# The third pair's attention weights transposed by the DMA engine inside the first block, and two later transfers moved behind stores

## The chip, the cores and the metric

One Trainium2 chip, one core. A core has TensorE (PE, the matmuls; its weight loads are listed apart as PEld), VectorE (DVE), ScalarE (ACT), GpSimd (POOL) and SyncE (SP, which issues nearly all DMA transfers here), and 16 DMA engines between the chip's memory and the core's on-chip memories SBUF and PSUM. Each engine works through its own list of instructions in order and waits at semaphores for the others. The metric is the device time of one execution in microseconds.

## The reference, cut to what matters

Two steps follow one another. Attention works on chunks of 64 tokens that see only themselves; a gated feed-forward layer (Mish) follows. Everything is float32.

```python
scores = scale * np.matmul(q_c, k_c.transpose(0, 1, 2, 4, 3))   # 8 batches, 8 heads, 9 chunks of 64 x 64
scores = scores - np.max(scores, axis=-1, keepdims=True)
attn = np.exp(scores)
attn = attn / (np.sum(attn, axis=-1, keepdims=True) + 1e-09)
out = np.matmul(attn, v_c)
...
h = x @ w_in                                   # x: 4608 tokens x 512; w_in: 512 x 2048
sp = np.where(h > 20.0, h, np.log1p(np.exp(np.minimum(h, 20.0))))
g = h * np.tanh(sp)
return (g @ w_out).astype(np.float32)          # w_out: 2048 x 512
```

## The kernel before, in words

The 4608 tokens are 36 tiles of 128; two tiles are a pair, 18 pairs in all, numbered from 0. A float32 factor of the large matmuls is split into an upper and a lower part ("hi" is a rounded copy by ACT, "lo" is the difference, made by DVE), and three matmuls stand for one.

**The first block.** The first eight tiles (pairs 0 to 3) go through two plain blocks of 16 slots each, slots 0 to 31. `prologue()` does the attention of pairs 0 and 1 and starts the first slots. Slot s of `slot()` issues to PE the up-projection of slot s+1 (`up`, tile h, line 389, 12 matmuls) and the down-projection of slot s-1 (`down`, tiles o, line 424, 12 matmuls), to ACT the Mish of slot s+1 (`mish`, line 401) and the upper part of slot s's activations (`g_hi`, line 406), and to DVE their lower part (`g_lo`, line 411). `down(s-1)` reads the lower part of slot s-1 first. In slots 0 to 15 the weights also have to be made: each slot loads two 512 KB tiles of raw weights over SP (`w("load")`, line 163), and ACT and DVE unpack and split them (`w_scale`, lines 170 and 179; `w_bits`, 192 and 193; `w_hi`, 205; `w_lo`, 211). `keep()` writes made weights back to memory.

The attention of pairs 2 and 3 lies between these steps; the table `softmax` says in which slot each step of which pair is issued: scores (`s`), maximum, exponential, sum with reciprocal (`a_inverse`, lines 310, 315, 318), division (`a_norm`, line 323, on DVE), transpose on PE (`a_transpose`, line 332, eight 128x128 tiles into PSUM) with a copy to SBUF by ACT (`a_copy`, line 342), and the product with the values (`a_values`, line 256, tile av), whose result ACT and DVE split into the block's x (`a_hi`, line 363; `a_lo`, line 366). Scores, transposes and values of one pair share one place in PSUM, so the next pair's transposes wait until `a_lo` has read the values. Pair 2 is divided in slot 8, transposed in slot 9 and multiplied in slot 10; pair 3 is transposed in slot 12 and multiplied in slot 13.

**The later blocks.** Four larger blocks of seven tiles each use a Strassen scheme: sets of 14 steps (`s_set`), in which PE alternates six matmuls of the up side (`s_up`, line 884) and six of the down side (`s_down`, tile d, line 1003). `s_out` adds the tile d to the totals in SBUF (line 1031, DVE) or, where a block begins anew, copies it there (line 1029, ACT). When a block is done, its totals go out in two groups of four stores (`s_store`, line 1047). Ten later pairs are spread over the sets by `plan_pair`. The distance from one pair's scores to its values decides between three plans: NEAR transposes on PE; MID and FAR let POOL separate the two 16-bit halves of each number (`p_split`, line 790), the DMA engine transpose them (`p_turn`, line 796, issued by SP), and POOL join them again (`p_join`, line 802). A pair has two such transfers, t = 0 and t = 1, of 128 x 1024 16-bit words. Two pairs follow FAR; their scores are at steps 92 and 204 and their second transfer is issued just ahead of the end of a block.

SP issues everything in one order, so a transfer also stands behind every transfer that was issued ahead of it.

## Time and profile before

| | |
|---|---|
| median of 3 runs | 795.67 us (794.31 to 795.96) |
| the profiled execution | 795.43 us, of which the span from the first to the last instruction is 793.6 us |
| PE busy | 780.8 us, 98% of the span |
| DVE busy | 591.8 us, 75% |
| ACT busy | 474.8 us, 60% |
| POOL busy | 302.7 us, 38% |
| q1, the queue of SP | 202.53 MB, 76.5% of the 16 DMA engines' span |

The difference between the profiled execution and its span, 1.8 us, is start and end, which the instructions don't show. A busy share is an average over stages in which different engines hold the others up; what a change is worth has to be read in the stage that it touches.

### The profile page before, as it was taken

How to read it: one execution, taken by the hardware profiler on the slowest of the kernel's cores; microseconds unless marked ns; L12 is line 12 of the kernel's file. 1: busy time of each engine (PE TensorE's matmuls, PEld its weight loads, DVE VectorE, ACT ScalarE, POOL GpSimd, SP SyncE). 2: the span in 40 equal slices, each digit the busy share in tenths (PEclk: the TensorE clock that was granted, in tenths of full speed). 3: DMA queues.
4: the chain of work that ended last, by engine and by line, in shares of the span. 5: the costliest groups of instructions: out<-in, count | busy, mean ns of one | idle time of the engine just before them, and what ended most of it. 6: DMA issues, size and time to landing. Idle time of an engine off the chain costs nothing.

```text
span 793.6 us, 15301 instructions
## 1 busy us (share of the span) xinstructions
PE 780.8 (98%) x5932; PEld 700.8 (88%) x5932; DVE 591.8 (75%) x929; ACT 474.8 (60%) x853; POOL 302.7 (38%) x263
## 2 busy tenths in 40 slices
PE   8999999999999999999999999999999999999996
PEld 7887888888889999999899999989999999999986
DVE  6898978888866776799577679976575897445666
ACT  5988865666676665555566466648464654544440
POOL 2000026556363236434434435454544453333340
PEclk9999999999999999999999999999999999999999
DMA  7698876989978868667978957788967667866537
GB/s 292 240 305 305 277 228 238 349 289 331 376 241 305 303 219 283 235 218 241 311 298 228 358 194 242 270 255 286 308 209 237 221 216 243 295 218 225 180 115 172
DMA packets 97224, 205.47 MB, mean 259 GB/s; under 512 B 26240, under 2 KB 49280, under 8 KB 89984
## 3 DMA queue, kind: packets, MB, share of 16 engines
q1 hardware_dynamic: 92864, 202.53, 76.5%
q10 hardware_dynamic: 4288, 1.97, 1.0%
q8 instruction: 47, 0.77, 0.4%
q14 instruction: 25, 0.20, 0.1%
HBM read 162.53 MB, written 38.80 MB: 254 GB/s over the span
## 4 chain that ended last, share of the span: by engine, by line
PE 76%; DVE 11%; ACT 6%; DMA 2%; issue 2%; SPq 1%; DVEq 0%; ACTq 0%
PE d L1003 29%; PE al L884 16%; PE g L884 8%; PE o_o L424 8%; PE h L389 7%; PE b L884 4%; PE av L256 2%; DVE sums L1031 2%; DVE sums L1034 1%; DMA out<-sums 1%; PE al L720 1%; DMA sums<-in_w_out 1%; DVE c L192 1%; DVE xo L211 1%; ACT c L170 1%
## 5 line engine op out<-in xcount | busy, mean ns | idle before, releaser
L1003 PE MATMUL d<-u,wo 128*128 128x448 f32 x796 | 203.9, 363 | 0.0
L1031 DVE TENSOR_TENSOR sums<-d,sums 128x448 f32<-128x448 f32 x192 | 118.6, 618 | 77.8 <-PE d L1003 77.6
L884 PE MATMUL al<-xo,ring 128*128 128x448 f32 x768 | 174.6, 362 | 0.0
L1003 PEld LDWEIGHTS d<-u,wo 128*128 128x128 f32 x796 | 148.6, 188 | 11.6 <-DVE u L963 0.6
L884 PEld LDWEIGHTS al<-xo,ring 128*128 128x128 f32 x768 | 143.3, 187 | 11.0 <-ACT sums L929 0.5
L884 PE MATMUL g<-xo,ring 128*128 128x448 f32 x384 | 87.6, 363 | 0.2 <-ACT y L929 0.2
L884 PEld LDWEIGHTS g<-xo,ring 128*128 128x128 f32 x384 | 71.6, 188 | 5.4 <-ACT y L929 0.6
L1003 PE MATMUL d<-yr,wo 128*128 128x448 f32 x192 | 56.7, 363 | 0.8 <-ACT sums L1029 0.8
L1003 PE MATMUL d<-xo,wo 128*128 128x448 f32 x182 | 55.0, 365 | 0.3 <-ACT sums L1029 0.3
L1003 PE MATMUL d<-g,wo 128*128 128x448 f32 x174 | 51.8, 363 | 0.2 <-DVE sums L1031 0.2
L953 ACT ACTIVATE b<-b 128x448 f32<-128x448 f32 x32 | 16.9, 528 | 52.0 <-DVE b L939 51.9
L640 POOL TENSOR_TENSOR c<-c 128x256 f32<-128x256 f32 x12 | 10.7, 898 | 97.5 <-DVE c L608 95.3
L884 PE MATMUL b<-xo,ring 128*128 128x448 f32 x192 | 43.6, 362 | 0.0
L953 ACT ACTIVATE y<-y 128x448 f32<-128x448 f32 x22 | 12.7, 577 | 48.1 <-DVE y L939 48.1
L985 POOL TENSOR_TENSOR z<-y,z 128x448 f32<-128x448 f32 x24 | 27.7, 1154 | 35.4 <-DVE y L985 21.9
L953 ACT ACTIVATE z<-g 128x448 f32<-128x448 f32 x32 | 17.4, 544 | 39.7 <-DVE g L939 31.1
L424 PE MATMUL o_o<-xo,g 128*128 128x512 f32 x168 | 40.9, 392 | 0.1
L389 PE MATMUL h<-x,xo 128*128 128x512 f32 x168 | 40.8, 392 | 0.0
L1003 PEld LDWEIGHTS d<-yr,wo 128*128 128x128 f32 x192 | 36.0, 188 | 3.6 <-ACT sums L1029 1.2
L884 PEld LDWEIGHTS b<-xo,ring 128*128 128x128 f32 x192 | 36.0, 188 | 2.5
L424 PEld LDWEIGHTS o_o<-xo,g 128*128 128x128 f32 x168 | 31.2, 188 | 6.6 <-DVE g L411 0.2
L389 PEld LDWEIGHTS h<-x,xo 128*128 128x128 f32 x168 | 31.2, 188 | 6.5
(265 smaller groups left out, 1660.8 us busy)
## 6 DMA issues: line engine op xcount, KB each, us to landing
ring<-dwi SPq DMA_DIRECT2D x56, 1024.0 KB, 7.2
wo<-dwo SPq DMA_DIRECT2D x112, 512.0 KB, 4.5
sums<-in_w_in SPq DMA_DIRECT2D x16, 512.0 KB, 5.2
sums<-in_w_out SPq DMA_DIRECT2D x16, 512.0 KB, 5.8
q<-in_q SPq DMA_DIRECT2D x16, 512.0 KB, 6.5
k<-in_k SPq DMA_DIRECT2D x16, 512.0 KB, 6.9
v<-in_v SPq DMA_DIRECT2D x16, 512.0 KB, 6.2
dwo<-sums SPq DMA_DIRECT2D x15, 512.0 KB, 5.2
```

The source lines that it names most:

```text
L170: nc.scalar.activation(out=c.bitcast(F32), in_=a[:, :, 1].bitcast(F32), func=AF.Copy, scale=2.0**-112)
L192: nc.vector.scalar_tensor_tensor(out=c, in0=c, scalar=3, in1=a[:, :, 0], op0=left, op1=either)
L211: engine.tensor_tensor(out=w_cols(m, w_dst(m, f, 1), True), in0=w_cols(m, wc.pop((m, f))["c"].bitcast(F32), False), in1=w_cols(m, w_dst(m, ...
L256: nc.tensor.matmul(o[h * CHUNK : (h + 1) * CHUNK, c, t - ts.start, g], lhsT=l[rows, t, 2 * g + h], rhs=r[rows, t, 2 * g + h], start=True, ...
L389: nc.tensor.matmul(h[:, cols], lhsT=wi(f, w_, kt), rhs=x[:, kt, cols], start=(n == 0), stop=(n == 3 * NK - 1),)
L424: nc.tensor.matmul(acc[t], lhsT=g[:, sl], rhs=w_part(f, w_), start=(f == 0 and n == 0), stop=(f == NF - 1 and n == 2),)
L640: nc.gpsimd.tensor_tensor(out=o, in0=a, in1=b, op=op)
L884: nc.tensor.matmul(o[:, :HALF], lhsT=w_[:, wn, kt * P : (kt + 1) * P], rhs=x[:, xn, kt], start=(n == 0 and k < 3), stop=(n == 5), skip_gro ...
L953: nc.scalar.activation(out=take(z, 12) if n == 12 else i, in_=i, func=AF.Mish)
L985: engine.tensor_tensor(out=o, in0=l, in1=r, op=ALU.subtract)
L1003: nc.tensor.matmul(o[:, :HALF], lhsT=wos[(len(DOWN) * y + kk) % 4][:, i, part, h * P : (h + 1) * P], rhs=x, start=(m == 0 and k in (5, 2, 1)),
L1031: nc.vector.tensor_tensor(out=o, in0=i, in1=o, op=ALU.add)
```

## The change

Pair 2 takes the way of the far pairs, but inside the first block. In slot 8 DVE now makes the lower part of slot 8's activations first and divides the pair behind it; POOL then splits each half of the pair into two planes of 16-bit words (`a_split`, two copies of 128 x 1024 words) into the room "early". In slot 9 SP issues the two transposing transfers (`a_turn`) between its two weight loads, and POOL joins the planes again into the same room (`a_join`, two copies). The eight transposes on PE and the copy by ACT are gone. The values of pair 2 are multiplied in slot 11 in place of slot 10, and with them `a_hi` and `a_lo`. The room of x1, which takes the place of "early", is opened behind these values (it was opened before slot 0). For the two FAR pairs the second transfer is issued at step 46 from their scores (it was 42), its join at step 53 (it was 50); the first transfer, and MID, stay where they were.

```diff
+    def words(x, t):
+        return x[:, t].bitcast(U16)
+
+    def a_split(j, x):
+        d = st[j]
+        d["x"] = x
+        d["w"] = d["p"].rearrange("p t g c k -> p t (g c k)")
+        for t in range(2):
+            nc.gpsimd.tensor_copy(
+                out=words(x, t).rearrange("p (b n) -> p b n", b=2),
+                in_=words(d["w"], t).rearrange("p (n b) -> p b n", b=2),
+            )
+
+    def a_turn(j):
+        d = st[j]
+        for t in range(2):
+            nc.sync.dma_start_transpose(
+                out=words(d["w"], t).rearrange("p (m n) -> p m n", n=P), in_=words(d["x"], t)
+            )
+
+    def a_join(j):
+        d = st[j]
+        for t in range(2):
+            nc.gpsimd.tensor_copy(
+                out=words(d["x"], t).rearrange("p (n b) -> p b n", b=2),
+                in_=words(d["w"], t).rearrange("p (b n) -> p b n", b=2),
+            )
+        d["ps"] = d["x"].rearrange("p t (h k) -> p t h k", k=CHUNK)
...
         "norm": {8: (2,), 9: (3,)},
-        "t": {9: (2,), 12: (3,)},
-        "v": {10: (2,), 13: (3,)},
+        "split": {8: (2,)},
+        "turn": {9: (2,)},
+        "join": {9: (2,)},
+        "t": {12: (3,)},
+        "v": {11: (2,), 13: (3,)},
...
         for j in a["v"]:
             a_values(j)
+            if j == 2:
+                x1_open()
...
         w("load", n + 4)
+        for j in a["turn"]:
+            a_turn(j)
+        for j in a["join"]:
+            a_join(j)
         if s:
             w("hi", n)
...
-        for j in a["norm"]:
-            a_norm(j)
+        if not a["split"]:
+            for j in a["norm"]:
+                a_norm(j)
...
             g_hi(s)
             g_lo(s)
+        for j in a["split"]:
+            a_norm(j)
+            a_split(j, view("early", 0, [2, DM]))
         if s + 1 < N:
             mish(s + 1)
...
-    MID = dict(exp=5, sum=(8, 9), norm=(10, 12))
-    FAR = dict(exp=33, sum=(36, 37), norm=(38, 40))
+    MID = dict(exp=5, sum=(8, 9), norm=(10, 12), turn=(12, 14), join=(20, 22))
+    FAR = dict(exp=33, sum=(36, 37), norm=(38, 40), turn=(40, 46), join=(48, 53))
...
-                m = start + n["norm"][t]
-                at_(m + 1, lambda t=t: p_split(j, t))
-                at_(m + 2, lambda t=t: p_turn(j, t))
-                at_(m + 10, lambda t=t: p_join(j, t))
+                at_(start + n["norm"][t] + 1, lambda t=t: p_split(j, t))
+                at_(start + n["turn"][t], lambda t=t: p_turn(j, t))
+                at_(start + n["join"][t], lambda t=t: p_join(j, t))
```

The lists of instructions, engine by engine, show where this puts things. DVE in slot 8 before, from the weights' bits to the sum of pair 3 (p_643 and r_0_863 are pair 2's weights and reciprocals, p_812 is pair 3; g is the lower part of the activations):

```order
L192 SCALAR_TENSOR_TENSOR c<-c,sums 128x512
L193 SCALAR_TENSOR_TENSOR c<-sums,c 128x512
L211 TENSOR_TENSOR xo<-c,xo 128x4x4x32
L323 TENSOR_TENSOR p_643<-p_643,r_0_863 128x2x8x64
L411 TENSOR_TENSOR g<-z,g 128x512
L192 SCALAR_TENSOR_TENSOR c<-c,sums 128x512
L193 SCALAR_TENSOR_TENSOR c<-sums,c 128x512
L211 TENSOR_TENSOR xo<-c,xo 128x512
L310 TENSOR_REDUCE r_0_913<-p_812 128x8x2
```

The same place after the change (p_638 is pair 2, p_807 pair 3; lines below 346 keep their numbers, later ones are 29 higher here):

```order
L192 SCALAR_TENSOR_TENSOR c<-c,sums 128x512
L193 SCALAR_TENSOR_TENSOR c<-sums,c 128x512
L211 TENSOR_TENSOR xo<-c,xo 128x4x4x32
L440 TENSOR_TENSOR g<-z,g 128x512
L323 TENSOR_TENSOR p_638<-p_638,r_0_858 128x2x8x64
L192 SCALAR_TENSOR_TENSOR c<-c,sums 128x512
L193 SCALAR_TENSOR_TENSOR c<-sums,c 128x512
L211 TENSOR_TENSOR xo<-c,xo 128x512
L310 TENSOR_REDUCE r_0_910<-p_807 128x8x2
```

Only the division and the lower part have changed places; DVE has the same instructions up to the lower part of slot 9. POOL, which had nothing here, has its four copies from the end of this division on.

PE in slots 9 to 11 before (h are the up-projections of slots 10, 11 and 12, o the down-projections of slots 8, 9 and 10):

```order
L389 MATMUL h_920<-x_89,xo 128x512 x12
L332 MATMUL pt_0_933<-ident,p_643 128x128 x8
L424 MATMUL o_o_489<-xo,g 128x512 x6
L424 MATMUL o_o_490<-xo,g 128x512 x6
L389 MATMUL h_977<-x_89,xo 128x512 x12
L256 MATMUL av_0_990<-ps_962,v_814 64x64 x32
L424 MATMUL o_o_489<-xo,g 128x512 x6
L424 MATMUL o_o_490<-xo,g 128x512 x6
L389 MATMUL h_1056<-x_89,u 128x512 x12
L424 MATMUL o_o_489<-xo,g 128x512 x6
```

The same place after the change:

```order
L418 MATMUL h_917<-x_89,xo 128x512 x12
L453 MATMUL o_o_484<-xo,g 128x512 x6
L453 MATMUL o_o_485<-xo,g 128x512 x6
L418 MATMUL h_967<-x_89,xo 128x512 x12
L453 MATMUL o_o_484<-xo,g 128x512 x6
L453 MATMUL o_o_485<-xo,g 128x512 x6
L418 MATMUL h_1011<-x_89,u 128x512 x12
L256 MATMUL av_0_1024<-early,v_809 64x64 x32
L453 MATMUL o_o_484<-xo,g 128x512 x6
L453 MATMUL o_o_485<-xo,g 128x512 x6
```

The transposes (pt) are gone, and the values (av) stand one up- and one down-projection later, behind the down-projection of slot 9.

SP around the second transfer of a FAR pair at the end of a block before (wo and ring are loads of weights, `out<-sums` the stores, `c<-x` the second transfer):

```order
L796 DMA_TRANSPOSE c<-c 128x8x128
L869 DMA wo<-dwo_114 128x1024
L864 DMA ring<-dwi_105 128x2048
L796 DMA_TRANSPOSE c<-x_1419 128x8x128
L869 DMA wo<-dwo_114 128x1024
L1047 DMA out<-sums 32x14x128 x4
L869 DMA wo<-dwo_114 128x1024
L1047 DMA out<-sums 32x14x128 x4
```

The same place after the change:

```order
L825 DMA_TRANSPOSE c<-c 128x8x128
L898 DMA wo<-dwo_114 128x1024
L893 DMA ring<-dwi_105 128x2048
L898 DMA wo<-dwo_114 128x1024
L1076 DMA out<-sums 32x14x128 x4
L825 DMA_TRANSPOSE c<-x_1414 128x8x128
L898 DMA wo<-dwo_114 128x1024
L1076 DMA out<-sums 32x14x128 x4
```

The transfer has passed one load of weights and the first four stores, and is still ahead of the second four. The other FAR pair reads alike.

## Rows read from the trace of the kernel before

**Rows 1.** The page's busy times: engine, busy us, share of span, instructions.
```profile
PE 780.8 (98%) x5932; PEld 700.8 (88%) x5932; DVE 591.8 (75%) x929; ACT 474.8 (60%) x853; POOL 302.7 (38%) x263
```

**Rows 2.** The chain of waits, 55 to 110 us: start, us, what.
```profile
71.13 0.69 DVE xo L211
...
83.62 0.61 DVE g L411
```

**Rows 3.** Timeline, 62 to 102 us: start, us, engine, line, [idle before <-releaser].
```profile
75.24 1.22 DVE L323 TENSOR_TENSOR p<-p,r 128x1024 f32<-128x1024 f32 x1
...
76.60 1.06 PE L332 MATMUL pt<-ident,p 128*128 128x128 f32 x8 [0.69 <-DVE p L323]
...
82.41 1.22 DVE L323 TENSOR_TENSOR p<-p,r 128x1024 f32<-128x1024 f32 x1
...
84.28 3.06 PE L424 MATMUL o_o<-xo,g 128*128 128x512 f32 x12
...
89.89 2.88 PE L424 MATMUL o_o<-xo,g 128*128 128x512 f32 x12
...
91.42 1.22 DVE L366 TENSOR_TENSOR x<-av,x 128x1024 fp32r<-128x1024 f32 x1
...
95.34 1.03 PE L332 MATMUL pt<-ident,p 128*128 128x128 f32 x8
```

**Rows 4.** Timeline of PE, 95 to 111 us, around pair 3's values.
```profile
98.95 2.88 PE L389 MATMUL h<-x,u 128*128 128x512 f32 x12
...
105.71 2.88 PE L389 MATMUL h<-x,u 128*128 128x512 f32 x12
```

**Rows 5.** Timeline of POOL and DVE at 125, 130 and 428 us.
```profile
124.94 0.74 POOL L640 TENSOR_TENSOR c<-z 128x256 f32<-128x256 f32 x1 [3.48 <-DVE z L608]
...
130.57 1.83 DVE L662 TENSOR_TENSOR sums<-c,sums 128x512 fp32r<-128x512 f32 x2
130.72 1.12 POOL L640 TENSOR_TENSOR z<-z,c 128x256 f32<-128x256 f32 x1 [1.79 <-DVE z L608]
...
428.25 1.04 POOL L790 COPY c<-c 128x1024 uint16<-128x1024 uint16 x1
...
428.99 0.84 DVE L760 TENSOR_TENSOR c<-c,r 128x512 f32<-128x512 f32 x1
```

**Rows 6.** Lines 790 and 802, POOL's copies: ns min/median/max.
```profile
L790 POOL COPY c<-c x6: 1036/1036/1038, 301.3 to 590.2; 128x1024 uint16<-128x1024 uint16 x6
L802 POOL COPY x<-c x6: 1337/1342/1361, 314.1 to 603.0; 128x1024 uint16<-128x1024 uint16 x6
```

**Rows 7.** The page's DMA issues: count, (KB each,) median us to landing.
```profile
sums<-in_w_out SPq DMA_DIRECT2D x16, 512.0 KB, 5.8
...
c<-c SPq DMA_TRANSPOSE x6, 3.2
c<-x SPq DMA_TRANSPOSE x6, 7.0
```

**Rows 8.** Timeline where a block ends, with a transfer ahead (380) and without (666).
```profile
379.98 4.27 SPq L1047 DMA_DIRECT2D out<-sums  x4
...
387.84 0.53 ACT L1029 COPY sums<-d 128x448 f32<-128x448 f32 x1 [2.83 <-DMA out<-sums]
...
666.48 3.64 SPq L1047 DMA_DIRECT2D out<-sums  x4
...
673.20 0.53 ACT L1029 COPY sums<-d 128x448 f32<-128x448 f32 x1 [0.46 <-DMA out<-sums]
```

**Rows 9.** Whom PE and its weight loads waited for: us in total, times, longest.
```profile
PE d L1003 <- ACT sums L1029: 1.1, 2, 0.8
...
PEld d L1003 <- ACT sums L1029: 1.8, 2, 1.2
```

**Rows 10.** Stretches: from:to, length, busy us of PE, PEld, DVE, ACT, POOL, then PEclk.
```profile
783.00:788.00 5.00, 4.05 (x21) 3.45 (x19) 4.86 (x9) 0.00 (x0) 0.00 (x0) 1.00 0.97 188
788.00:793.60 5.60, 0.00 (x0) 0.00 (x0) 0.39 (x1) 0.00 (x0) 0.00 (x0) 0.76 0.68 135
```

More of the change, by code (lines that the diff above doesn't have):

```diff
@@ L1291 @@
         prologue()
-        x1_open()
         for s in range(N - 1):
```

## The prediction

> **What bounds the kernel now.** The busy times come first: PE works for 98% of the span, no other engine for more than 75% [rows 1]. Most of the kernel is a row of matmuls without a gap, and whatever delays PE there delays the end. So I looked for the places where the chain of waits leaves PE, and the change touches two of them.
>
> The first is slots 7 to 9 of the first block. Here the chain is DVE's, without another engine, from 71.13 us (the lower part of a weight) to the lower part of slot 9's activations at 83.62 + 0.61 = 84.23 us [rows 2], and PE's down-projection of slot 9 starts at 84.28 [rows 3]. DVE has no gap in these 13.1 us. PE's only idle time in them, 0.69 us ahead of pair 2's transposes (they wait for the division) [rows 3], is therefore not a loss that can be taken back: with the transposes gone, PE is only earlier at a down-projection that DVE has not made ready. From 84.28 on PE is the chain, up to the end of a later block.
>
> The second is the end of two blocks. There ACT may not overwrite the totals before they are stored; it waits 2.83 us at 387.84, against 0.46 us at the third such place, which has no transfer ahead [rows 8]. PE waits twice for these copies, 1.1 us in sum by its matmuls and 1.8 us by its weight loads [rows 9].
>
> **Slots 8 to 12, step by step.** I use before's clock.
>
> Transposes, their wait, and ACT's copy removed: worth nothing, because DVE's chain covers them. Without that cover it would be the wait of 0.69 us and the eight transposes, which take 1.06 with their overlap into the next matmul [rows 3]: about 1.6 us.
>
> Division behind the lower part: the lower part of slot 8 is now ready at 75.24 + 0.68 = 75.92, so PE goes on at once. But DVE's instructions up to the lower part of slot 9 are the same ones, so 84.23 stays. PE does two phases of 12 matmuls, which take 95.34 - 89.89 = 5.45 us together [rows 3], from 76.0 to 81.4, and then stands.
>
> Values moved from slot 10 to slot 11: before, they lay under DVE's chain; now they lie behind it. The price is the two phases with pair 3's values against two without: (105.71 - 98.95) - 5.45 = 1.3 us [rows 3, 4]. All of it is on PE's path, and nothing behind it can hide it.
>
> Pair 3's transposes now have `a_lo` of pair 2 close ahead of them: it ran from 91.42 to 92.64 and they started at 95.34 [rows 3]. One slot (5.45 us) later, less the 1.2 us that it no longer takes in slot 10, it ends at 96.9; PE comes at 95.34 + 1.3 = 96.6. I take 0.3 us, with bounds of 0 and, if DVE gains nothing in slot 10, 1.5.
>
> POOL's copies are the disputed cost. The trace has the same copies elsewhere, 1.04 us a split and 1.34 us a join [rows 6], but nowhere beside such DVE work: behind the division stand instructions that read two operands from SBUF, one right after the other. The nearest row for that is at 130.57 [rows 5]: two such instructions in 1.83 us, where a first and a last of them stand on the chain with 0.69 and 0.61 [rows 2], 1.30 together, so DVE lost 0.5. POOL's instruction beside them took 1.12 us and takes 0.74 by itself [rows 5]: it waited 0.4 for the first of the two and then held up the second for most of its own length. The other row is one of DVE at 428.99 that began 0.3 us before the end of a split and took 0.84 in place of 0.69 [rows 5]: 0.15 lost. So a copy gets in between two DVE instructions and DVE stands until it ends. Here both splits are ready when DVE's chain is dense, so I take a split's length less 0.15: 2 x 0.9 = 1.8 us. Bounds: 2 x 0.15 = 0.3, and 2 x 1.34 = 2.7 if these splits go at the joins' pace. No reason allows a gain.
>
> The Trainium skill (SBUF — State Buffer, Who interferes with whom) says that a VectorE instruction with two inputs in SBUF contends with a GpSimd instruction that reads SBUF, and that whichever is issued first keeps the shared pair of ports for its whole instruction while the other is blocked. The rows agree as far as they go. By the rule the sum takes each copy at its whole length, by the row at 428.99 alone it would be 1.5 us less.
>
> So the lower part of slot 9 comes at 86.0. The joins wait for the transfers. SP can issue these behind a weight load; the median transfer of such a load takes 5.8 us, a transfer alone 3.2, one with other loads ahead 7.0 [rows 7]. Issued near 80 they land near 85, and DVE divides pair 3 from 82.41 + 1.8 = 84.2 to 85.4. Whether the first join (1.34) gets in ahead of the lower part of slot 9 is a toss-up: 0 or 1.3 us, I take 0.4. What comes later of the joins falls on DVE while PE has two phases and the values to do (6.8 us), and costs 0 to 0.3.
>
> Sum of this part: 1.3 + 0.3 + 1.8 + 0.4 = +3.8 us. Without any hold-up of DVE it is +1.6.
>
> **The end of the two blocks.** The second transfer leaves the place ahead of the first four stores. From the first store's issue to ACT's copy it is 387.84 - 379.98 = 7.9 us with the transfer ahead and 673.20 - 666.48 = 6.7 us without [rows 8], so the copy comes 1.2 us earlier, as much as the longer of PE's waits (0.8 by matmuls, 1.2 by weight loads [rows 9]). I take 1.4 us for both, between 1.1 and 1.8. The transfer is then late by some 6 us, but its join, three steps (3.6 us) later, is still ahead of the pair's values by a step or two. If it isn't, PE waits there for what it gained; so 0 to -1.8.
>
> Together: +3.8 - 1.4 = +2.4 us, on 795.43 us of the profiled execution (0.24 below the median): 797.8 us.
>
> **The rivals.**
> 1. *POOL costs DVE little* (it gets in under the sum over pair 3, which reads one operand, or DVE keeps the port): +1.6 - 1.4 = +0.2, 795.6 us. For it: at 428.99 DVE lost only 0.15 us. Against: at 130.57 POOL came between two DVE instructions [rows 5].
> 2. *DVE isn't the bound in slots 7 to 9*: then transposes and wait come off, -1.6, the values cost nothing new, and with the blocks' ends -1.4 it is -3.0: 792.4 us, faster. It takes DVE to reach the lower part of slot 9 by 82.6, 1.6 us earlier than now. Against it: DVE's list up to there has lost nothing, and the chain shows no gap.
> 3. *PE's clock falls.* PE would stand from 81.4 to 86.0 or 87.3, 4.6 to 5.9 us. In the trace PE's last matmuls end about 787 us (4.05 us of work in the stretch from 783), the granted clock is 1.00 up to 788 and 0.76 on average from there to the end, where PE has nothing to do [rows 10]: it fell from 2.4 to 1.2 GHz while PE stood. That stand is about as long as mine would be. At half the clock the two phases (5.45 us) behind the stand would take twice as long; I bound it by 0 to 3 us more, 798 to 801.
>
> The Trainium skill (TensorE: Matmul & The Clock Gate, What's actually happening) says that an idle TensorE falls back to half its clock and regains it after sustained work. No run here shows it in mid-kernel.
>
> 4. *The blocks' ends give nothing* (the second four stores or the join are late instead): +3.8, 799.2 us.
>
> **How the numbers follow.** 0.2% is 1.6 us, about what a measurement of this kernel can tell from no change. My forecast (POOL holds DVE up, +1.7 to +3.0): 0.40. Rival 1: 0.22; rival 2: 0.08; rival 3: 0.16; rival 4: 0.08; something else of either sign: 0.06. Range: from rival 1's 795 to the middle of rival 3's, 800.5. Faster by over 0.2% is rival 2 and half of the rest: 0.10. Same is rival 1 and the low end of the forecast: 0.30. Slower: 0.60.
>
> **What the profile after would show.** Right: DVE's weight instructions behind the division stretched or gapped by about a microsecond each beside two POOL copies; PE idle for over 4 us ahead of the down-projection of slot 9; no wait of ACT over 1 us for stores at 387 and 535. Wrong: the same DVE instructions at 0.69 us and that down-projection at 84.3 or earlier. What would make me wrong most: an arbitration in which POOL waits for DVE.

## The result, and the profile after

The changed kernel takes 800.77 us (median of 4, 800.54 to 801.31) against 795.67: a ratio of 1.0072, 95% interval 1.0059 to 1.0085. That is 5.1 us slower, above the range given. A second set of runs, made later, gave 800.34 against 795.58 (1.0061, 1.0047 to 1.0075). The profiled execution has a span of 798.8 us, 5.2 more than before.

The page's busy times hardly move (PE 780.8 us before [rows 1]):

```profile
PE 783.4 (98%) x5924; PEld 701.4 (88%) x5924; DVE 595.4 (75%) x929; ACT 474.5 (59%) x852; POOL 309.3 (39%) x267
```

The timeline after, 74 to 101.5 us (start, us, engine, line, [idle before <-releaser]; lines above 346 are 29 higher than before, so L440 is the lower part, L453 the down-projection, L418 the up-projection, L395 the lower part of pair 2's values; lines between these are left out):

```profile
77.06 2.71 POOL L355 COPY early<-p 128x1024 uint16<-128x1024 uint16 x2 [54.07 <-DVE p L323]
77.46 1.41 DVE L193 SCALAR_TENSOR_TENSOR c<-sums,c 128x512 uint32<-128x512 uint32 x1
78.79 1.52 DVE L211 TENSOR_TENSOR xo<-c,xo 128x512 fp32r<-128x512 f32 x1
84.87 0.68 DVE L440 TENSOR_TENSOR g<-z,g 128x512 fp32r<-128x512 f32 x1
84.89 3.54 POOL L370 COPY early<-p 128x1024 uint16<-128x1024 uint16 x2 [5.12 <-DMA p<-early]
85.47 1.76 DVE L192 SCALAR_TENSOR_TENSOR c<-c,sums 128x512 uint32<-128x512 uint32 x1
85.60 5.49 PE L453 MATMUL o_o<-xo,g 128*128 128x512 f32 x12 [4.04 <-DVE g L440]
87.27 1.65 DVE L193 SCALAR_TENSOR_TENSOR c<-sums,c 128x512 uint32<-128x512 uint32 x1
90.89 3.21 PE L418 MATMUL h<-x,u 128*128 128x512 f32 x12
94.02 1.16 PE L256 MATMUL av<-early,v 64*64 64x64 f32 x64
95.11 3.02 PE L453 MATMUL o_o<-xo,g 128*128 128x512 f32 x12
99.40 1.22 DVE L395 TENSOR_TENSOR x<-av,x 128x1024 fp32r<-128x1024 f32 x1
100.69 1.07 PE L332 MATMUL pt<-ident,p 128*128 128x128 f32 x8
```

Three things stand here. The two DVE instructions beside the splits take 1.41 and 1.52 us, the two beside the joins 1.76 and 1.65; 0.69 is their length alone, so DVE loses 1.55 and 2.03 us. PE stands 4.04 us, and the 12 matmuls behind the stand take 5.49 us in place of 3.06 [rows 3]. And the lower part of pair 2's values ends at 99.40 + 1.22 = 100.62; pair 3's transposes start right behind it, at 100.69, against 95.34 before [rows 3]. That PE shows no wait there is a coincidence, as the runs below tell: two paths end at this place within about 0.2 us of each other. One is DVE's list; the other is PE itself behind its stand, and the chain of waits of this profile goes by the second one (start, us, what):

```profile
84.95 0.61 DVE g L440
85.60 5.49 PE o_o L453 x12
...
100.85 0.91 PE pt L332 x8
```

The stretches around the stand (from:to, length, busy us of PE, PEld, DVE, ACT, POOL with the number of instructions, then PEclk, the busy share of the DMA engines and their GB/s):

```profile
78.00:81.00 3.00, 3.00 (x15) 2.35 (x14) 3.00 (x3) 1.27 (x3) 1.77 (x2) 1.00 0.83 249
81.00:85.50 4.50, 0.56 (x3) 0.13 (x1) 4.40 (x9) 3.38 (x7) 0.61 (x1) 0.91 1.30 242
85.50:88.00 2.50, 2.40 (x6) 1.92 (x7) 2.47 (x3) 0.00 (x0) 2.50 (x2) 0.50 0.66 245
88.00:91.00 3.00, 3.00 (x9) 2.32 (x8) 2.97 (x5) 2.05 (x4) 0.43 (x1) 0.50 0.85 236
91.00:94.00 3.00, 3.00 (x13) 2.19 (x11) 2.96 (x6) 3.00 (x6) 0.00 (x0) 0.92 0.83 233
```

The granted clock went from 2.4 to 1.2 GHz while PE stood and came back soon after 91 us.

PE's lateness against before, by the starts of its groups, can be followed through the block:

| PE starts | before | after | late by | what was added |
|---|---|---|---|---|
| down-projection of slot 9 | 84.28 | 85.60 | 1.32 | DVE's lower part is late |
| up-projection behind it | 87.17 | 90.89 | 3.72 | 2.40: half the clock |
| down-projection of slot 10 | 89.89 | 95.11 | 5.22 | 0.41 clock, 1.09 values |
| pair 3's transposes | 95.34 | 100.69 | 5.35 | 0.13: the phase behind the values |

So the first block loses 5.4 us in this execution. The two block ends were to give 1.4 back. They are read from SP's and ACT's timeline and from the list of waits (us in total, times, longest):

```profile
385.43 3.50 SPq L1076 DMA_DIRECT2D out<-sums  x4
389.05 3.41 SPq L825 DMA_TRANSPOSE c<-x  x1
...
393.28 0.53 ACT L1058 COPY sums<-d 128x448 f32<-128x448 f32 x1 [2.82 <-DMA out<-sums]
...
539.90 0.53 ACT L1058 COPY sums<-d 128x448 f32<-128x448 f32 x1 [3.02 <-DMA out<-sums]
...
PEld d L1032 <- ACT sums L1058: 1.4, 2, 0.8
...
PE d L1032 <- ACT sums L1058: 0.7, 2, 0.5
```

The transfer is behind the stores now, but ACT's copy still waits 2.82 us, 393.28 - 385.43 = 7.85 us after the first store against 7.86 before [rows 8]. At the second block end it waits 3.02 us. PE's waits fell from 1.1 to 0.7 us by matmuls and from 1.8 to 1.4 by weight loads [rows 9]: 0.4 us in place of 1.4.

### The profile page after: what moved, and what is told of

Its sections match the earlier page's. It is cut to its first block, busy times and chain, and to the rows that moved or that the text cites. A ratio compares the mean times of both kernels' runs of the same rounds, so it can differ in the third digit from the quotient of the medians.

```text
span 798.8 us, 15294 instructions
## 1 busy us (share of the span) xinstructions
PE 783.4 (98%) x5924; PEld 701.4 (88%) x5924; DVE 595.4 (75%) x929; ACT 474.5 (59%) x852; POOL 309.3 (39%) x267
## 4 chain that ended last, share of the span: by engine, by line
PE 76%; DVE 10%; ACT 7%; DMA 3%; issue 2%; SPq 0%; ACTq 0%; DVEq 0%
PE d L1032 28%; PE al L913 16%; PE o_o L453 8%; PE g L913 8%; PE h L418 7%; PE b L913 4%; PE av L256 2%; DMA sums<-in_w_out 2%; DVE sums L1060 2%; DMA out<-sums 2%; DVE sums L1063 1%; ACT c L170 1%; PE al L749 1%; ACT sums L179 1%; DVE c L789 1%
## 5 line engine op out<-in xcount | busy, mean ns | idle before, releaser
L453 PE MATMUL o_o<-xo,g 128*128 128x512 f32 x168 | 43.5, 410 | 4.0 <-DVE g L440 4.0
L453 PEld LDWEIGHTS o_o<-xo,g 128*128 128x128 f32 x168 | 32.8, 198 | 11.7 <-DVE g L440 4.7
L418 PE MATMUL h<-x,xo 128*128 128x512 f32 x168 | 41.0, 392 | 0.0
L418 PEld LDWEIGHTS h<-x,xo 128*128 128x128 f32 x168 | 31.1, 188 | 6.7 <-DVE xo L211 0.2
L1032 PEld LDWEIGHTS d<-xo,wo 128*128 128x128 f32 x182 | 34.0, 187 | 3.3 <-ACT sums L1058 0.6
```

What stands on the lines that cost most here:

```text
L418: nc.tensor.matmul(h[:, cols], lhsT=wi(f, w_, kt), rhs=x[:, kt, cols], start=(n == 0), stop=(n == 3 * NK - 1),)
L453: nc.tensor.matmul(acc[t], lhsT=g[:, sl], rhs=w_part(f, w_), start=(f == 0 and n == 0), stop=(f == NF - 1 and n == 2),)
L1032: nc.tensor.matmul(o[:, :HALF], lhsT=wos[(len(DOWN) * y + kk) % 4][:, i, part, h * P : (h + 1) * P], rhs=x, start=(m == 0 and k in (5, 2, 1)),
```

## The experiments

Each run has its own runs of the kernel before beside it (795.4 to 795.8 us). "Late" below is against the kernel before.

### The stand, its clock, and the transposes of pair 3

Four corners: with and without the clock's fall, with and without the wait of pair 3's transposes.

**The clock away.** 15 matmuls more ahead of the down-projection of slot 9; nobody reads their result.

```diff
+        if s == 10:
+            o = HOME[0].tile([P, 2, 2, NG, CHUNK], F32, name="fill", tag=HOME[1])
+            for _ in range(15):
+                nc.tensor.matmul(
+                    o[:, 0].rearrange("p t g k -> p (t g k)"),
+                    lhsT=wi(11, 0, 0),
+                    rhs=xts[0][:, 0][:, 0, :TOK],
+                    start=True,
+                    stop=True,
+                )
         if 1 <= s < N - 1:
             down(s - 1)
```

> The changed kernel, with 15 more matmuls on PE ahead of the down-projection of slot 9, into a PSUM place that nobody reads; they give PE some 3.4 us of work in its stand of 4.04 us and take nothing out. Theory (the clock): the part of the loss that the sum did not hold is PE's granted clock, 0.50 from about the end of the stand to about 91.4 us, so that the 12 matmuls took 5.49 us and the up-projection behind them 3.21. Then the clock stays at 1.00 here, the down-projection takes 2.9 us, and the time falls by about 2.8 us, to 798.0. Rival (other work beside it): the down-projection is slow because of what runs beside it, POOL's two joins from 84.9 to 88.4 us and DVE's stretched instructions, which stay as they are; then it still takes over 4 us and the time stays at 800.8.

Measured: 800.48 us (ratio 1.0059, 1.0047 to 1.0072), though the granted clock stayed at 1.00 from 78 to 94 us and the slow 12 matmuls were gone. PE's timeline:

```profile
81.48 3.57 PE L1136 MATMUL fill<-x,xo 128*128 128x512 f32 x15
86.76 3.06 PE L453 MATMUL o_o<-xo,g 128*128 128x512 f32 x12 [1.70 <-DVE g L440]
...
100.73 1.09 PE L332 MATMUL pt<-ident,p 128*128 128x128 f32 x8 [1.44 <-DVE x L395]
```

The theory had the clock's cause right and its worth wrong. The 12 matmuls are fast again, although the joins still run beside them, so nothing but the clock had made them slow. But in this execution a join came in ahead of the lower part of slot 9 (1.2 us later), and pair 3's transposes wait 1.44 us for the lower part of pair 2's values and start at 100.73, where they started with the slow clock. So DVE's list alone, without any slow matmul, is enough to bring these transposes to 100.7: two bounds end in one place.

**Both away.** Pair 3's transposes, besides, behind the down-projection of slot 11.

```diff
-        for j in a["t"]:
-            a_transpose(j)
...
         if 1 <= s < N - 1:
             down(s - 1)
+        for j in a["t"]:
+            a_transpose(j)
```

> The changed kernel with the 15 matmuls in PE's stand again, and pair 3's transposes behind the down-projection of slot 11 in place of ahead of it. With the 15 matmuls alone the clock stayed at 1.00, but pair 3's transposes stood 1.44 us for the lower part of pair 2's values and began at 100.7 us, where they also began without the matmuls: two waits of one size in a row. Theory: with both taken away the time falls by that 1.44 us, from 800.5 to 799.0, and PE has no wait there. Rival (something later holds PE at the same place, DVE's lower parts above all): 800.5 again.

Measured: 798.18 us (1.0028, 1.0019 to 1.0038), 2.3 less than with the matmuls alone. More than the 1.44, since here no join came ahead of the lower part of slot 9; PE then has no wait at the transposes:

```profile
85.15 3.03 PE L453 MATMUL o_o<-xo,g 128*128 128x512 f32 x12 [0.62 <-DVE g L440]
...
100.22 1.03 PE L332 MATMUL pt<-ident,p 128*128 128x128 f32 x8
```

**The wait alone away.** The same move of the transposes without the 15 matmuls.

> The changed kernel with pair 3's transposes behind the down-projection of slot 11, and without the 15 matmuls in PE's stand: the fourth corner. Without the stand's clock alone: 800.5; without that and the transposes' wait: 798.2. Theory (two bounds of nearly one size side by side: PE's slow clock from 85 to 91 us, and DVE's chain up to pair 3's transposes; taking one away gives nothing): the clock still falls, the down-projection of slot 9 takes over 4 us, and the time stays at 800.3 to 800.8. Rival (DVE's chain alone was the bound and the 15 matmuls were beside the point): 798.2.

Measured: 798.98 us (1.0047, 1.0035 to 1.0059). Neither theory nor rival: it is 1.4 to 1.8 us less than the changed kernel. PE's timeline:

```profile
84.83 4.62 PE L453 MATMUL o_o<-xo,g 128*128 128x512 f32 x12 [4.04 <-DVE g L440]
89.28 2.92 PE L418 MATMUL h<-x,u 128*128 128x512 f32 x12
```

The stand is the same 4.04 us, but the slow clock behind it was shorter in this execution: 4.62 and 2.92 us for the two phases, in place of 5.49 and 3.21. That is 1.2 us which the moved transposes, issued after both, did not bring. So this corner is not clean: how much of the 1.4 to 1.8 us is the wait and how much the shorter fall isn't shown. Taking away the clock's fall alone gave nothing, the wait alone at most 1.8 us, both together 2.6 (800.77 - 798.18).

### DVE's chain

**The values alone.** The kernel before, with pair 2's values in slot 11.

```diff
-        "v": {10: (2,), 13: (3,)},
+        "v": {11: (2,), 13: (3,)},
```

> The kernel before with one edit: the values of pair 2, and the two instructions that split their result, in slot 11 in place of slot 10; the transposes stay on PE. Theory: before, the values lay under DVE's chain and cost nothing; now PE stands about 1.2 us ahead of the down-projection of slot 9, which starts at 84.3 as before, and the values cost 1.2 to 1.3 us behind it: 796.9. Rival 1: they cost nothing in slot 11 either (something else in slots 11 to 13 has room): 795.7. Rival 2: already a stand of 1.2 us makes the clock fall: a down-projection of over 4 us, and 798 or more.

Measured: 797.91 us (1.0027, 1.0016 to 1.0038), 2.5 late. PE's timeline shows, besides the stand of about 1.2 us that the theory had, a wait that it did not have:

```profile
84.10 3.03 PE L424 MATMUL o_o<-xo,g 128*128 128x512 f32 x12 [1.14 <-DVE g L411]
...
97.00 1.09 PE L332 MATMUL pt<-ident,p 128*128 128x128 f32 x8 [0.39 <-DVE x L366]
```

Behind the stand of 1.14 us the 12 matmuls keep their 3.03 us, and pair 3's transposes wait 0.39 us: the room of 2.7 us that lay there before (95.34 against 91.42 + 1.22 [rows 3]) is used up by the shift alone. Whatever DVE loses ahead of this place is from now on lost by PE, unless something else is later still.

**POOL's copies alone.** Four copies in the kernel before, behind pair 2's division, whose result nobody reads; the third and fourth go from one half of the room "early" to the other.

```diff
+    def pool_copies(j):
+        x = view("early", 0, [2, DM])
...
+        for t in range(2):
+            nc.gpsimd.tensor_copy(
+                out=words(x, t).rearrange("p (b n) -> p b n", b=2),
+                in_=words(p, t).rearrange("p (n b) -> p b n", b=2),
+            )
+        for t in range(2):
+            nc.gpsimd.tensor_copy(
+                out=words(x, 1 - t).rearrange("p (n b) -> p b n", b=2),
+                in_=words(x, t).rearrange("p (b n) -> p b n", b=2),
+            )
...
             a_norm(j)
+            if j == 2:
+                pool_copies(j)
```

> The kernel before with four POOL copies added behind pair 2's division, in the form of the change's two splits and two joins and into the same room, whose result nobody reads (the room of x1 is opened behind pair 2's values, as in the change). No transfer, no pair moved, the transposes on PE as before. Theory (POOL's copies hold DVE up by about 0.75 us a split and 1.0 us a join): the lower part of slot 9 comes 3.4 us later, near 87.6, and there is nothing to hide it: 799.0, more if the clock falls in the stand. Rival (the copies get in beside DVE without a loss): 795.6.

Measured: 799.3 us (1.0052, 1.0039 to 1.0064), 3.7 late. The timeline of DVE, POOL and PE (lines between are left out):

```profile
75.58 2.71 POOL L352 COPY early<-p 128x1024 uint16<-128x1024 uint16 x2 [53.49 <-ACT sums L179]
75.87 1.52 DVE L192 SCALAR_TENSOR_TENSOR c<-c,sums 128x512 uint32<-128x512 uint32 x1
77.43 1.41 DVE L193 SCALAR_TENSOR_TENSOR c<-sums,c 128x512 uint32<-128x512 uint32 x1
78.35 3.42 POOL L357 COPY early<-early 128x1024 uint16<-128x1024 uint16 x2
78.76 1.78 DVE L211 TENSOR_TENSOR xo<-c,xo 128x512 fp32r<-128x512 f32 x1
80.46 1.21 DVE L310 TENSOR_REDUCE r<-p 128x16 f32<-128x1024 f32 x1
...
85.83 4.58 PE L439 MATMUL o_o<-xo,g 128*128 128x512 f32 x12 [1.91 <-DVE g L426]
```

Three instructions with two operands in SBUF lose 0.83, 0.72 and 1.09 us; the fourth copy falls beside the sum over pair 3, which reads one operand and takes its usual 1.21 us. So DVE loses 2.64 us. PE pays with its stand of 1.91 us and with a slow clock behind it: the 12 matmuls take 4.58 us in place of 3.06, so about 1.5 us of this kernel's loss is the clock's.

**Both together.** The same copies in the kernel with the values moved.

> The same four POOL copies in the kernel before with pair 2's values in slot 11 (797.9 without them). So it has the two things that the change adds to the first block, and none of what it takes away: the transposes and ACT's copy are still there, and no transfer is. Theory (the change's loss is the shift of the values and POOL's hold-up of DVE, one behind the other on DVE's chain to pair 3's transposes): 797.9 + 3.2 to 3.4 = 801.2. Rival (the loss needs the transfers, the order of the division or the place in the SP queue): 797.9 to 799.

Measured: 800.84 us (1.0068, 1.0055 to 1.008), 5.3 late. This kernel takes nothing away, has no transfer in the first block and no edit at the block ends, and it is as slow as the changed kernel. So neither the transfers nor the order of the division is needed for the loss. But it comes there by another path than the theory had. PE's and ACT's timeline:

```profile
87.53 4.61 PE L439 MATMUL o_o<-xo,g 128*128 128x512 f32 x12 [3.80 <-DVE g L426]
...
96.08 1.01 ACT L378 CAST x<-av 128x1024 fp32r<-128x1024 f32 x1 [0.90 <-PE av L256]
```

All four copies fall ahead of the lower part of slot 9 here, the slow clock follows PE's stand of 3.80 us, and ACT waits 0.90 us for PE's values: PE's slow matmuls, and not DVE's list, lead to pair 3's transposes. That the time is the forecast one is in part luck. What the run does show of the transposes of pair 2, which PE still does here: they lie ahead of the stand, so that without them PE would only stand longer.

**The sum and the division of pair 3 later.**

```diff
-        "sum": {7: (2,), 8: (3,)},
-        "norm": {8: (2,), 9: (3,)},
+        "sum": {7: (2,), 9: (3,)},
+        "norm": {8: (2,), 10: (3,)},
```

> The changed kernel with the sum over pair 3 in slot 9 in place of 8 and its division in slot 10 in place of 9. The lower part of slot 9 has 2.7 us less of DVE's work ahead of it and comes near 82.9 us, so PE stands 1.4 us in place of 4.0 and the clock has no reason to fall; but DVE has the same instructions as before up to the lower part of pair 2's values. Theory (DVE's chain up to pair 3's transposes is the bound): those still start near 100.7, PE's wait goes there, and the time is 800.3 to 800.8. Rival (what counts is the stand ahead of the down-projection of slot 9 and the clock behind it): 1.3 us of hold-up and 2.8 of clock come off, 796.7.

Measured: 801.21 us (1.0068, 1.0054 to 1.0081). PE's timeline:

```profile
81.81 3.01 PE L453 MATMUL o_o<-xo,g 128*128 128x512 f32 x12 [1.31 <-DVE g L440]
...
90.09 3.02 PE L453 MATMUL o_o<-xo,g 128*128 128x512 f32 x12 [1.46 <-DVE g L440]
...
98.52 1.09 PE L332 MATMUL pt<-ident,p 128*128 128x128 f32 x8 [2.69 <-DVE x L395]
99.37 4.58 PE L453 MATMUL o_o<-xo,g 128*128 128x512 f32 x12
```

The stand of 4.04 us is cut to 1.31, and PE waits 1.46 and 2.69 us for DVE at two later places, as the theory said in kind: PE waits for the same list of DVE's work wherever it is cut. The rival's 796.7 is refuted. But the time is above the theory's range too. The sum over pair 3 now lies beside a join and loses nothing by it (DVE's timeline):

```profile
84.72 1.21 DVE L310 TENSOR_REDUCE r<-p 128x16 f32<-128x1024 f32 x1
```

So DVE's list is 1.1 us shorter up to pair 3's transposes (98.52 against 100.69, counted from the division of pair 2 at 74.52 and 75.61), and the slow clock behind the last wait, 4.58 us for 12 matmuls, takes this back.

**The copies on ACT.** First the two splits, then all four (the joins then in slot 10 in place of slot 9).

```diff
-            nc.gpsimd.tensor_copy(
+            nc.scalar.copy(
```

> The changed kernel with the two splits of pair 2 made by ACT in place of POOL; the joins stay on POOL. After the change DVE's L193 and L211 beside the splits took 1.41 and 1.52 us in place of 0.69 each (1.55 us lost), and the two instructions beside the joins 1.76 and 1.65 (2.05 lost). Theory (one DVE chain up to pair 3's transposes, which wait for the lower part of pair 2's values): the 1.55 us come back at the lower part of slot 9 (about 84.0 us) and at the transposes (99.1 in place of 100.7): 799.2. Rival 1 (POOL's copies are not what stretched DVE): the same DVE instructions stay long beside ACT, 800.8. Rival 2: ACT's two copies delay the Mish and the upper parts by their own 2 us: 801 to 803.

Measured: 800.97 us (1.0064, 1.0051 to 1.0076). ACT's and DVE's timeline:

```profile
75.89 2.00 ACT L355 COPY early<-p 128x1024 uint16<-128x1024 uint16 x2 [2.73 <-DVE p L323]
...
78.92 0.69 DVE L211 TENSOR_TENSOR xo<-c,xo 128x512 fp32r<-128x512 f32 x1 [1.73 <-ACT xo L205]
```

Rival 1 is refuted, and rival 2 has the mechanism, at the lower edge of its range: DVE's instructions are back at 0.69 us beside ACT's copies, so POOL had stretched them; but the upper part of a weight now stands behind these copies on ACT, and DVE waits 1.73 us for it in place of the 1.55.

> The changed kernel with all four copies of pair 2 made by ACT in place of POOL, the joins in slot 10 behind its first weight. Theory (POOL's copies held DVE up by 1.55 + 2.05 = 3.6 us, on the chain that ends at pair 3's transposes): DVE's instructions are back at 0.69 us each, the lower part of slot 9 comes at 84.0, that of pair 2's values near 97.0, ahead of PE; the values' 1.2 us stay: 796.5, and up to 799.3 if the clock still falls in a stand of about 2.5 us. Rival (the room is lost elsewhere: ACT's copies take the place of POOL's on the same chain): 800 or more.

Measured: 800.47 us (1.0067, 1.0054 to 1.0081): the rival, by the same wait of 1.73 us and a second one, for the upper part of slot 10's activations, which now stands behind the joins on ACT (DVE's timeline):

```profile
92.07 0.69 DVE L440 TENSOR_TENSOR g<-z,g 128x512 fp32r<-128x512 f32 x1 [2.30 <-ACT g L435]
```

**The transposes back on PE.**

```diff
-        d["ps"] = d["x"].rearrange("p t (h k) -> p t h k", k=CHUNK)
...
-        "t": {12: (3,)},
+        "t": {9: (2,), 12: (3,)},
```

> The changed kernel with pair 2's transposes on PE and the copy by ACT put back in slot 9; the splits, transfers and joins stay, but their result is not used. The prediction gave the transposes, their wait and the copy 0 us, under the cover of DVE's chain. By that: PE works 0.8 us more, waits for the division at 76.8, stands less ahead of the down-projection of slot 9, which starts when DVE's lower part is there, and the time stays at 800.8 (or less, to 800.0, if the shorter stand leaves more of the clock). Rival: the 1.6 us that they would cost without cover come on top: 802.4.

Measured: 804.06 us (1.0105, 1.0092 to 1.0119), and it says nothing on the question: ACT's copy of the transposes waited 5.83 us for POOL's joins, a wait that neither the kernel before nor the changed one has.

```profile
87.31 1.01 ACT L342 COPY ps<-pt 128x1024 f32<-128x1024 f32 x1 [5.83 <-POOL early L370]
```

### The block ends

**The edit on the far pairs undone, and done alone.** The changed kernel with `turn=(40, 42), join=(48, 50)` for FAR; and the kernel before with `turn=(40, 46), join=(48, 53)`.

> The changed kernel without its edit on the two far pairs: their second transfer is issued at step 42 and joined at step 50 again. The prediction gave the edit -1.4 us: then 802.2. The trace after shows the first ACT copy after the first block end 5.44 us later than before and the one after the second 5.13 us later, against 5.42 us ahead of both: -0.3 to -0.4 in sum, so 801.1. Rival: nothing at all, 800.8.

> The kernel before with the edit on the two far pairs alone (second transfer at step 46, join at 53). As the prediction had it: -1.4 us, 794.3. As the trace after has it: -0.3 to -0.4, 795.3, with ACT's waits for the stores still about 2.8 and 3.0 us. Rival: nothing, 795.7.

Measured: 799.66 us (1.0049, 1.0035 to 1.0062), and 793.74 us (0.998, 0.9971 to 0.9989). On the kernel before the edit gives 1.7 us, the 1.4 of the prediction and some more; PE's wait by matmuls is down to one:

```profile
PE d L1003 <- ACT sums L1029: 0.2, 1, 0.2
```

The gain doesn't come at both ends as the prediction had it. From the first store to ACT's copy it is 7.79 us at the first end (7.86 before) and 7.41 at the second (8.42 before), so only the second copy comes clearly earlier.

In the changed kernel the edit gives nothing. To have both beside each other they ran once more:

> The changed kernel as it is, beside the next run on the same chip: 800.8.

> The changed kernel without its edit on the far pairs once more, now beside the changed kernel on the same chip. On the kernel before the edit gave -1.7 us (795.4 to 793.7). If it gives the same behind the changed first block, this kernel takes 802.4; the first run of it took 799.7, by which the edit costs 1.1 us there. Theory: what the edit is worth depends on where the loads stand when the stores come, which the first block shifts, so between 799.7 and 801.5; rival: the first run was an accident and this one is 802 or more.

Measured: 800.34 us with the edit, 799.72 without (1.0054, 1.0041 to 1.0067). The intervals overlap, but a gain of 1.4 is excluded. The two profiles are further ones of the same first block (the one with the edit is of an execution of 804.76 us, far above the median), as is that of the first run without the edit, and they show how much one execution differs from the next: in two of the four a join comes in ahead of the lower part of slot 9 and PE stands 5.1 us in place of 4.04, and the 12 matmuls behind take 4.62 to 5.49 us. Pair 3's transposes wait for DVE (0.24 us) in one of the four; in the others PE itself is the last.

**No second transfer.** In the kernel before, the far pairs' second half is copied without its transposition.

```diff
+                if n is MID or t == 0:
                     at_(start + n["turn"][t], lambda t=t: p_turn(j, t))
                     at_(start + n["join"][t], lambda t=t: p_join(j, t))
+                else:
+                    at_(start + n["join"][t], lambda t=t: p_keep(j, t))
```

> The kernel before without the second transfer of the two far pairs; their second half is copied in place of joined, so its weights are not transposed. It shows what the transfer at the end of the blocks costs at most. If the transfer ahead of the first four stores is what makes ACT wait there, PE's two waits by matmuls (0.28 and 0.81 us) and the longer ones by weight loads go: 794.2, 1.1 to 1.8 less than 795.6. Rival: the stores' own landing (0.7 us more or less from kernel to kernel, also at the third such place that has no transfer) makes the waits: 795.2 or more.

Measured: 793.29 us (0.997, 0.9959 to 0.998), without a wait of PE for these copies. So the transfer is what PE pays for at the block ends of the kernel before: 2.5 us (1.6 to 3.3 by the interval), somewhat more than its waits there of 1.1 and 1.8 us, and step 46 gets back about two thirds of that.

**The transfer behind all stores,** at step 49, the join at 54.

> The kernel before with the second transfer of the far pairs at step 49, behind both groups of stores, and its join at 54, two steps ahead of the values. In the change (step 46) the transfer stands right behind the fourth store, and this store landed 1.2 to 1.8 us behind the third, against 0.4 to 1.5 with the transfer ahead. Theory (a transfer right behind a store still slows it): at step 49 PE waits for no copy at the first place of either block, and the time is that of the kernel without the transfer, about 794.0. Rival 1: the same as with step 46, 793.7. Rival 2: the transfer or the join is now late, PE waits ahead of the values at the two far pairs: 795.5 to 797.

Measured: 806.07 us (1.0137, 1.0121 to 1.0152): PE waits for the join ahead of the values, 4.20 us at the first of the two places and 3.61 at the second.

```profile
394.96 1.14 PE L256 MATMUL av<-x,v 64*64 64x64 f32 x32 [4.20 <-POOL x L802]
```

### A version to beat both

The kernel before with the far pairs' edit, and in slots 8 and 9 the lower part ahead of the division, pair 2's transposes behind the down-projection of slot 8.

```diff
+        for j in a["t"]:
+            if j == 2:
+                a_copy(j)
+        for j in a["norm"]:
+            a_norm(j)
         if s + 1 < N:
             mish(s + 1)
```

> The kernel before with the far pairs' edit and, in the first block, DVE's lower part ahead of the division in slots 8 and 9, pair 2's transposes behind the down-projection of slot 8, and ACT's copy of them behind the upper part of slot 9. Nothing is added and no pair is moved to another slot. Theory (DVE's chain up to the lower part of slot 9 is what PE waits for): this part comes 1.2 us earlier, at 83.0, PE has its 0.69 us wait no more and is just done with the values: 1.0 to 1.2 us less than with the far pairs' edit alone (793.7), so 792.6. Rival: ACT's later copy delays the values or the next weights by as much: 793.7 to 795.

Measured: 794.66 us (0.9986, 0.9972 to 0.9999). PE's wait only went from the transposes to the down-projection ahead of them, 0.59 us. The lowest time of a kernel that does all the work is that of the one before with the far pairs' edit alone, 793.74 us.

## Why the prediction was wrong

**Division behind the lower part, transposes removed: 0.** Nothing speaks against it: the kernel that has both additions and keeps the transposes on PE is as slow, and there they lie ahead of a stand of 3.80 us. The run that was to price the transposes by themselves gave no answer.

**Values behind DVE's chain: +1.3.** Right: 1.09 us for the values and 0.13 in the phase behind them (5.35 - 5.22 in the table). The 0.3 for pair 3's transposes is right too where POOL adds nothing: with the values moved alone they wait 0.39 us.

**POOL holds DVE up ahead of the lower part of slot 9: +1.8, first join +0.4.** Right in kind, somewhat large: 1.55 us in two instructions, PE late by 1.32. Whether a join comes in ahead was called a toss-up, and it is one: in this execution none does, in two of the four profiles with this first block one does. The Trainium skill (SBUF — State Buffer, Who interferes with whom) says that a VectorE instruction with at most one input in SBUF, outside the two-port modes, does not contend with GpSimd, and that one with two contends with a GpSimd instruction that reads SBUF. The traces agree with both halves (1.21 us for the sum beside a copy and without one, 1.41 to 1.78 in place of 0.69 for the others). That the first keeps the ports for its whole instruction, as the prediction quotes it, the same section of the Trainium skill spells out for the two-port modes. For two inputs these traces come close to it: a split, 1.04 us alone, cost DVE 0.72 and 0.83.

**What comes later of the joins "falls on DVE while PE has two phases and the values to do (6.8 us), and costs 0 to 0.3"; pair 3's transposes +0.3, at most 1.5.** This is the step that failed. The joins cost DVE 2.03 us, and PE's work does not cover them, because DVE's own chain goes on past the lower part of slot 9 to the lower part of pair 2's values, for which pair 3's transposes wait. The prediction had this chain's end right without POOL (96.9 us against PE at 96.6) and so had it at zero room, but added POOL's hold-up only at slot 9. With all of it, 1.55 + 2.03 = 3.6, the sum from its own numbers is 96.9 + 3.6 = 100.5; the trace has 100.62, and the first block loses 5.35 us in place of the 3.8 forecast. The run with the clock at 1.00 shows that this chain is enough by itself: PE waits 1.44 us for it, and the time stays.

**The clock, rival 3: 0 to 3 us.** It fell as described, and held PE up by 2.8 us (2.40 + 0.41 in the table), by 1.7 where the wait alone was away. This path is the last one in the profile after, but DVE's chain ends beside it, so that it is no term of a sum: without it the changed kernel takes 0.3 us less, a difference within the interval. That the measured time lies in this rival's 798 to 801 is luck: it reached that far by adding the clock to a sum in which DVE's chain was short. The Trainium skill (TensorE: Matmul & The Clock Gate, What's actually happening) has TensorE at half its clock after idling. The trace agrees in mid-kernel too: the granted clock is 0.50 behind the stand.

**Block ends: -1.4.** This is the second step that failed. In time it is right for the kernel before (-1.7), though the gain is at one end and not at both; it is wrong for the changed kernel (0.4 by its waits, nothing by its time). Without the edit the changed kernel has PE waits of 0.57 us at one end in one profile and none in the other, against 0.28 and 0.81 before: there was less to win. With the edit it has 0.25 and 0.45 us in the profile after, and 2.05 at the second end in the later one. Why, stays open: the kernel with the values moved and POOL's copies is as late when it comes there and waits 0.40 and 0.94 us.

It took both failed steps to leave the range. With the first block at +5.35 and the ends at -1.4 the time would be 799.4, with +3.8 and nothing from the ends (rival 4) 799.2; both lie inside. With both it is 795.43 + 5.35 = 800.8.

**The other rivals.** That POOL costs DVE little is refuted by the copies alone (2.64 us on DVE, 3.7 in time). That DVE isn't the bound in slots 7 to 9 is refuted by the stand of 4.04 us, which waits for DVE's lower part until 85.55 us, where the rival needed 82.6. Of what the profile after was to show, the stretched DVE instructions and a stand of over 4 us are there; ACT's waits of under 1 us for the stores are not (2.82 and 3.02).

In sum: +2.5 for the lower part and the values, +2.8 for DVE's chain behind them (and the clock beside it), -0.3 for the ends and the rest: about +5.1. The -0.3 is what is left over, not a measurement.

## What to carry to other kernels

A chain of waits that leaves an engine does not mean that this engine is free from there on: before adding work to it, follow its list to the next place where the others wait for it, and note the room there. Here it was 2.7 us, and moving one product by a slot used all of it, so that hold-up before it was no longer hidden. Two bounds that end at the same place hide each other: take one away, and the time may not move.

## What was not expected of the hardware

POOL slows down with DVE: the two splits took 2.71 us and the two joins 3.54, against 2 x 1.04 and 2 x 1.34 alone [rows 6]. SP takes 3.41 us at one block end and 2.86 at the other to issue a transposing transfer right behind four stores. The same transfer ahead of them, in the kernel before, takes 1.50 and 1.73 (SP's timeline of the first):

```profile
376.70 1.50 SPq L796 DMA_TRANSPOSE c<-x  x1
```
